# A recurrence with a gated feed-forward layer: another table for the order of its parts

## The chip, the cores and the metric

The kernel runs on one core of a Trainium2 chip. Its metric is the device time in microseconds (us) of one execution, taken as the median of several. Five engines work side by side, each through its own list of instructions, strictly in order: TensorE (PE, with PEld for the loading of its stationary operand), VectorE (DVE), ScalarE (ACT), GpSimd (POOL) and SyncE (SP), which issues every transfer of this kernel. An instruction whose input isn't there stops everything that stands behind it in the same list.

## What is computed

The first half is a linear-attention recurrence over 768 steps, for 4 batches of 8 heads with a head dimension of 40:

```python
for t in range(S):
    y[:, :, t] = einsum('bhd,bhde->bhe', r[t], state)
    Sa = einsum('bhde,bhe->bhd', state, a[t])
    state = state * w[t] - outer(Sa, b[t]) + outer(v[t], k[t])
```

The second half takes the result as rows of 320 values, x of shape (4, 768, 320):

```python
h = maximum(x @ w_in, 0)                 # 320 -> 1024
conv = a three-tap convolution of h along the sequence, per channel
out = (h * sigmoid(conv)) @ w_out        # 1024 -> 320
```

All of it is float32; inputs that arrive as 64-bit floats (the three weights) are turned into pairs of a high and a low part on the chip.

## The kernel before

The sequence is cut into 24 steps of 32 positions. Two steps make a pair (12 pairs, `pd`), for which the inputs w, a, k and b are loaded together, and two steps make a window of 64 positions (12 windows, `wd`) for the feed-forward layer. Within a step the recurrence is solved in closed form. The kinds of parts, each a Python generator whose `yield`s cut it into pieces, are:

- `weights` (token we, 23 parts, lines 208 to 320): loads a block of a weight matrix, turns it from 64-bit floats into a high and a low part with eight VectorE instructions (L217 to L235 on tiles such as `wo2q`), one ScalarE copy (L253) and one GpSimd subtraction (L255).
- `wakb`, `v`, `r` (ld, lv, lr): loads on the SP queue.
- `decays` and `decayed` (de, dd, one for each half of a pair): TensorE transposes w, a, k and b (L349), ScalarE shifts w into `wx` (L365, L366), VectorE scans it into running products `suf` and `pre` (L369, L376) and multiplies the transposed tiles into `ah`, `kt` and `bt` (L391, L399).
- `scores` and `hats` (sc, ha): TensorE products of the decayed tiles (L411), masked by VectorE into `at` (L437), and transposes back (L450).
- `solve_in` and `solve` (si, so, one for each pair): a triangular system of 32 unknowns is taken through DRAM into `bb` and solved by 31 pairs of instructions (L480 multiplies into `st`, L486 adds into `xx`). Pairs 0, 2, 4, 6, 8 and 10 are solved on VectorE, the odd ones on GpSimd. The result goes through DRAM into `tt` (L491, L496).
- `chain` (ch): the part that carries the state from step to step. TensorE multiplies the old state and v into `pp` (L514, L522), ScalarE copies it to `psb` (L527), TensorE applies the solution, `pu` (L533), ScalarE copies `u` (L538), TensorE builds the new state in `pn` (L549), VectorE adds the old one in four instructions (`s`, L562), and GpSimd scales it by the decay (L568).
- `rturn`, `vturn`, `uturn`, `sturn`, `pairs`, `outputs` and `finish` (rt, vt, ut, st, pa, ou, fi): the step's output. `pm` (L411) is masked by VectorE into `ms` (L614), `py` (L629, L638) is copied to `ysb` (L644), transposed to `pq` (L655) and multiplied by VectorE into `xf` (L657), which ScalarE and GpSimd split (L665, L667).
- `pack`, `moe_in` and `moe_out` (pk, mi, mo): the feed-forward layer. For each window there are four tiles `ph` of two blocks of 128 channels (16 matmuls, L700). ScalarE applies the maximum into `hb` (L714); VectorE copies the two columns at the border in from `hend` and out to it (L712, L716); ScalarE and VectorE do the three taps in `cc` (L721, L729), ScalarE the sigmoid (L734), VectorE the product (L736), ScalarE and GpSimd the split (L740, L743). Two tiles `po` of 24 matmuls (L754) follow for each window. `end` (en) does the last position.

The order of all this isn't left to a scheduler. The string `ORDER` at the top of the file is a list of tokens; `emit_all` reads it from left to right, and each token advances one part by one piece (`ch2` advances the chain of step 2 by one piece, `we13*2` weight block 13 by two). So a token's place fixes where its instructions stand in the list of every engine that it uses. `put` holds for each part what must have been issued before each of its pieces, and `advance` issues whatever is missing first; the semaphores that make the data safe come from the framework. There are 8 accumulator banks in TensorE's memory, six for the recurrence and two for the feed-forward layer.

```python
for token in ORDER.split():
    name, _, times = token.partition("*")
    numbers = [int(x) for x in name[2:].split(".") if x]
    for _ in range(int(times or 1)):
        advance((KINDS[name[:2]], *numbers))
```

Of the kernel before, what the change touches and what calls it, by code (L numbers as in the profile page):

```python
# [31 lines left out]
)  # L32

ORDER = """
    ld0 de0.0*2 ld0*2 de0.1 ld0 ld1 de0.1 we0 dd0.0*3 dd0.1*2 sc0 dd0.1 we0 ld1*2 lr0 sc0 sc1 lr1
    de1.0 sc1 ha0 de1.0 dd1.0 de1.1*2 we1*4 si0 ha0 ha1 dd1.0 we0*2 rt0 ld1 so0 ha1 dd1.0 so0 dd1.1
    ld2 so0*2 ld2 dd1.1 ld2 so0 dd1.1 ha2*2 sc2 ld2 lv0 lv1 vt0 ha3*2 so0*3 sc2 sc3 we2*2 sc3 we3
    we2*2 we3 we4 so0 we3*2 we5 we4 we5 si1 de2.0*2 ch0*4 we4*2 we6 lv2 de2.1*2 so1*2 ld3 ut0 pa0
    vt1 dd2.0*2 de3.0 we5 so1 we5 we7 ou0 we6 fi0 so1 dd2.0 ch1 we6 dd2.1 we7*2 ch1 we7 dd2.1*2 ld3
    st1*2 sc4 we6 so1 we8*4 we9 we10 ch1 lv3 rt1 we9 st1*2 ut1 pa1 lr2 ou1 ha4 ld3*2 we10 so1*3 fi0  # L40
    vt2 we10 fi0 fi1 de3.0 sc4 sc5 we9 we10 sc5 ch1 de3.1 we9 de3.1 ha4 we11 we12 lr3 rt2 fi1 st2*2
    fi1 we11 we12 we11*2 ro0 we13 we12*2 ha5 st2 we13 we14 ha5 ld4 so1 we13 dd3.0*3 dd3.1*3 we14*2
    ch2 si2 so2 ch2 pk0 ut2 so2*2 pa2 vt3 sc6 so2*2 st2 ou2 ch2 ro0 rt3 mi0.0*3 so2*2 mi0.0*2 ch2
    st3*2 we13 mi0.1*2 st3 ld4 so2 ld4 we14 lv4 we15 we16 ch3*2 sc6 sc7 ut3 we15 st3 we15 sc7 fi2*3
    lr4 mi0.0 pa3 mi0.0 ch3 we15 ch3 we16 mi0.0 we17 mi0.1 mi0.2 we17*2 mi0.2 so2 ch4 si3 we16 so3
    ou3 ha6 we16 we18 de4.0 we18 ha6 ha7 st4 fi3*2 we17 we19 de4.0 we18 mi0.1 we19 vt4 st4*3 lv5
    de4.1 ch4 ut4 so3 ch4 dd4.0 rt4 we18 we20 de4.1 we20 mi0.2 so3 we20 pa4 vt5 ch4 ch5 so3 mi0.2
    ch5 fi3 ha7 we19*2 we21*2 ut5 we20 we22*2 ou4 st5*2 mi0.1 st5 lr5 rt5 so3 we22 ld4 ld5 de5.0
    mi0.1 we21 ch5 we22 mi0.3 we21 mi0.0*2 so3 mi0.1*2 mi0.3 pa5 mi0.3 pk1 dd4.0*2 dd4.1 mi0.1*2
    dd4.1 st5 mi0.2 sc8 fi4*2 ld5 dd4.1 ou5 mi0.2 lv6 mi0.3 so3*2 sc8 mi0.2 sc9 mi0.2*2 ha8*2 ha9  # L50
    fi4 fi5 ld5 de5.0 de5.1 ha9 sc9 mi0.2 dd5.0 mi0.3 dd5.0 de5.1 lv7 mi1.0*3 mi1.1 ld5 dd5.0 dd5.1
    sc10 so3 si4 mi0.3 lr6 dd5.1*2 ch5 mi0.3 lr7 mi0.3 mi1.1*2 mi1.0*3 mi1.1 mi1.2 vt6 sc10 mi0.3
    mo0.0 sc11 mi0.3 mi1.1 mi1.0*2 mi1.1 ch6 st6 mi1.2 ch6*2 sc11 mi1.1*2 mo0.0*2 ch6 mo0.0 mo0.1*5
    ld6 ut6 rt6 ch7 mi1.1 so4 ld6 so4*2 pa6 vt7 st6 fi5*2 st6 so4*2 mi1.0 so4 mi1.2 st6 mi1.3 so4
    mi1.2 so4 lv8 ou6 mi1.0 mo1.0 mi1.2 mi1.3*2 st7*2 ch7 ut7 mi1.1 st7*2 rt7 ch7*2 mo1.0 pa7
    mi1.3*2 fi6*2 pk2 lr8 mi1.2*2 ou7 mi1.2 rt8 so4 si5 ch8 st8*2 mi1.2 mi1.3 mi1.2 mi1.3 ch8*2 lv9
    fi6 mi2.0*2 lr9 ld6 ch8 ha10*2 fi7 mi1.3*2 ha11 ld6 de6.0 vt8 lv10 de6.0 dd6.0 fi7 mi2.0 mi1.3
    mi2.1 ch9 mo1.0 mi2.0*2 de6.1 ch9 de6.1 so5*2 mi2.1 so5 mi2.0 ut8 mi2.1*4 mi2.0 mo0.0 mo1.0*2
    mo1.1 ha11 mi2.0 mi2.1 mo1.1 dd6.0 mo1.1 dd6.0 pa8 vt9 mo1.1 mi2.0*2 dd6.1 so5 fi7 st8*2 mi2.1*2
    dd6.1 so5 ou8 rt9 mi2.2 sc12 mi2.2*2 mi2.3*3 ut9 dd6.1 st9 mi2.1 mi2.2 ch9 mi2.2 mi2.3*2 mi2.2*2  # L60
    ld7 de7.0 lr10 ld7*2 so5*3 pa9 ch9 lr11 st9*3 pk3 ld7 mi2.3 mi2.2 mi3.0*2 mi2.3 mi3.0 mi2.3 fi8
    so5 fi8 mi2.2*2 mi2.3 mi3.0 ou9 mi3.1 fi8 sc12 fi9 de7.0 dd7.0 sc13 mo2.0*2 sc13 de7.1*2 mi3.1*2
    rt10 ha12*2 ha13 dd7.0 ha13 dd7.0 mi2.3 mi3.0 dd7.1*3 ch10 mi3.1*2 mi3.0 mi3.1 st10 fi9 mo2.0*2
    mo2.1 ch10*3 mo2.1 mi3.0 st10 mi3.1 st10*2 mi3.0 mi3.1 ut10 si6 so6 mi3.2*2 so6 lv11 vt10 mi3.2
    pa10 vt11 so6 mo1.1 so6 mi3.3 mo2.1 mi3.3 ch11 mo2.0 mo2.1 ld8 mi3.0 lr12 so6 ch11 so6 ou10 rt11
    mi3.3 mi3.1 ut11 pa11 st11*3 ld8 lv12 so6 mi3.2 mi3.3 st11 so6 sc14 ch11 vt12 mi3.1 lr13 sc14
    mi3.0 mo3.0 mi3.2 sc15 mi3.2 ch11 mi3.2 fi9 fi10 mi3.3 fi10*2 ou11 st12 ha14 sc15 mi3.2*2 mi3.3
    pk4 so6 ch12 mi3.2 de8.0 mi4.0*2 mi3.3 fi11*2 mi3.3 ch12*2 mo3.0 mi3.3*2 ch12 mi4.0*2 ut12 si7
    so7*2 mi4.1*2 fi11 mi4.1*2 lv13 mi4.0 ha14 st12 ha15 st12*2 mi4.0 mo3.0*2 mo3.1 mi4.1 rt12
    mi4.1*2 mi4.2 mo3.1 pa12 mo2.1 mo3.1*2 de8.0 so7 ld8 ch13 mi4.0*2 vt13 mi4.0*2 de8.1 dd8.0 mi4.2  # L70
    ou12 rt13 so7*2 mi4.2*2 mo3.0 so7*3 ch13 mi4.3 ld8 mi4.1*3 mi4.3 ld9 ch13 ha15 ut13 lv14 mi4.3
    pk5 mo3.1 fi12 de8.1 lr14 fi12 dd8.0*2 de9.0 dd8.1 ld9 dd8.1*2 sc16 mi4.2 st13*4 ld9*2 pa13
    mi5.0 mi4.2*3 mi5.0*2 mi4.2 mi5.0 mi4.2 ch13 mi4.3 ou13 ha16*2 sc16 sc17 fi12 fi13 ha17*2 de9.0
# [929 lines left out]
```

## Time and profile before

| | before |
|---|---|
| median of 3 executions | 708.97 us (708.5 to 709.71) |
| the profiled execution | 708.08 us |
| its span, from the first to the last instruction | 706.4 us |
| granted TensorE clock, mean | 0.906 |

The profile page and the answers of the trace come from that one execution. A row of the timeline gives the start in us from the span's start, how long it took, the engine, the line, the operation and its tiles without their numbers; in brackets behind it stands how long the engine sat idle just before, and who ended that wait. A row of the stretches gives, for a window of time, the busy time of each engine and the number of its instructions.

### The profile page before, as it was taken

Reading aid. Unit: us, or ns where it says so; the run is one execution under the profiler, and the core shown is the slowest. Engines: PE = TensorE matmul, PEld = TensorE weight load, DVE = VectorE, ACT = ScalarE, POOL = GpSimd, SP = SyncE. Lnnn points to the kernel's source line nnn. Section 1 sums busy time; section 2 is a strip of 40 time slices with the busy share of each in tenths; the row PEclk is TensorE's granted clock in tenths of the full one; section 3 lists DMA queues with packets and bytes.
Section 4 is the critical chain, followed back from the end, with each engine's and each line's share of the span. In section 5 each row is a group of like instructions: output and inputs, shape, how many; then the busy total and the mean of one; then the engine's idle time right before and its main releaser. Section 6 shows DMA issues by size and latency. Waiting matters only on the chain. (4 is left out here: it accounts for less than half of the span.)

```text
span 706.4 us, 29930 instructions
## 1 busy us (share of the span) xinstructions
PE 560.7 (79%) x13021; PEld 497.9 (70%) x13021; DVE 538.4 (76%) x1261; ACT 350.7 (50%) x792; POOL 353.2 (50%) x582
## 2 busy tenths in 40 slices
PE   4444764677687898988977996899998977899886
PEld 3334654566576787977866885789887876788775
DVE  6689889998999896657795578987979894456571
ACT  2322244254375455664454664466565546455651
POOL 2001884037786235783234884236985028863321
PEclk9766777997799998989999998999998999999998
DMA  8765456437125344544404446524435025121000
GB/s 139 120 117 108 103 112 102 95 94 144 22 41 107 56 72 79 94 81 82 82 20 89 86 86 106 81 60 69 89 62 91 6 54 94 29 51 32 21 30 19
DMA packets 242402, 53.40 MB, mean 76 GB/s; under 512 B 229000, under 2 KB 238112, under 8 KB 242272
## 3 DMA queue, kind: packets, MB, share of 16 engines
q1 hardware_dynamic: 242272, 51.50, 39.9%
q8 instruction: 102, 1.67, 1.0%
q14 instruction: 28, 0.23, 0.1%
HBM read 38.63 MB, written 10.22 MB: 69 GB/s over the span
## 5 line engine op out<-in xcount | busy, mean ns | idle before, releaser
L729 DVE SCALAR_TENSOR_TENSOR cc<-hb,cw,cc 128x256 f32<-128x256 f32 x192 | 106.3, 575 | 13.7 <-ACT cc L721 10.2
L568 POOL TENSOR_TENSOR s<-s,wc 120x360 f32<-120x360 f32 x88 | 75.8, 891 | 69.4 <-DVE s L562 69.4
L486 POOL TENSOR_TENSOR xx<-xx,st 128x126 f32<-128x126 f32 (+22 forms) x186 | 83.1, 447 | 14.6
L480 POOL TENSOR_TENSOR st<-xx,bb 128x126 f32<-128x126 f32 (+22 forms) x186 | 79.4, 427 | 21.1 <-DMA bb<-bd 8.4
L700 PE MATMUL ph<-xh,wih 120*128 120x256 f32 x288 | 56.6, 306 | 11.3 <-ACT hb L714 11.3
L486 DVE TENSOR_TENSOR xx<-xx,st 128x126 f32<-128x126 f32 (+22 forms) x186 | 54.2, 291 | 6.4
L480 DVE TENSOR_TENSOR st<-xx,bb 128x126 f32<-128x126 f32 (+22 forms) x186 | 53.6, 288 | 7.2 <-DMA bb<-bd 1.7
L736 DVE TENSOR_TENSOR cc<-cc,hb 128x512 f32<-128x512 f32 x48 | 40.8, 857 | 21.7 <-ACT cc L734 21.5
L562 DVE TENSOR_TENSOR s<-pn,s 120x360 f32<-120x360 f32 x88 | 40.6, 522 | 20.6 <-PE pn L549 20.6
L700 PEld LDWEIGHTS ph<-xh,wih 120*128 120x128 f32 x288 | 41.8, 194 | 15.0 <-ACT hb L714 13.1
L734 ACT ACTIVATE cc<-cc 128x512 f32<-128x512 f32 x48 | 30.4, 636 | 43.6 <-DVE cc L729 43.5
L667 POOL TENSOR_TENSOR xl<-xf,xh 120x384 fp32r<-120x384 f32 x24 | 26.8, 1117 | 45.2 <-ACT xh L665 41.5
L721 ACT ACTIVATE cc<-hb,cw 128x256 f32<-128x256 f32 x96 | 43.5, 506 | 8.7 <-DVE hb L712 2.9
L602 PE MATMUL pt<-ident,s 120*120 120x120 f32 x276 | 40.6, 279 | 6.4 <-DVE s L562 3.2
L427 ACT ACTIVATE ap<-ah,hmask 120x384 f32<-120x384 f32 (+1 forms) x72 | 36.6, 576 | 17.4 <-DVE ah L391 10.1
L604 ACT COPY sn<-pt 120x360 f32<-120x360 f32 x92 | 38.9, 471 | 12.2 <-PE pt L602 11.8
L714 ACT ACTIVATE hb<-ph 128x512 f32<-128x512 f32 x48 | 28.8, 600 | 27.2 <-PE ph L700 23.4
L579 ACT ACTIVATE rp<-pr,hmask 120x384 f32<-120x384 f32 x72 | 36.7, 586 | 6.9 <-PE pr L576 6.5
L700 PE MATMUL ph<-xl,wih 120*128 120x256 f32 x192 | 39.3, 287 | 0.0
L533 PE MATMUL pu<-psb,tt 32*32 32x40 f32 x1536 | 22.5, 209 | 19.6 <-ACT psb L527 16.1
L602 PEld LDWEIGHTS pt<-ident,s 120*120 120x120 f32 x276 | 31.2, 143 | 9.0 <-DVE s L562 3.5
L533 PEld LDWEIGHTS pu<-psb,tt 32*32 32x32 f32 x1536 | 18.7, 114 | 24.5 <-ACT psb L527 17.7
(867 smaller groups left out, 1665.9 us busy)
## 6 DMA issues: line engine op xcount, KB each, us to landing
bb<-bd SPq DMA_DIRECT2D x24, 256.0 KB
w<-in_w_dram SPq DMA_DIRECT2D x24, 160.0 KB
a<-in_a_dram SPq DMA_DIRECT2D x24, 160.0 KB
k<-in_k_dram SPq DMA_DIRECT2D x24, 160.0 KB
b<-in_b_dram SPq DMA_DIRECT2D x24, 160.0 KB
r<-in_r_dram SPq DMA_DIRECT2D x96, 40.0 KB
v<-in_v_dram SPq DMA_DIRECT2D x96, 40.0 KB
out_dram<-ob SPq DMA_DIRECT2D x22, 160.0 KB
```

The source lines that it names most:

```text
L480: eng.tensor_tensor(t3, xx[:, 0:nj, i : i + 1].to_broadcast([128, nj, nt]), bb[:, i : i + 1, i + 1 :].to_broadcast([128, nj, nt]), ALU.mult,)
L486: eng.tensor_tensor(xx[:, 0:nj, i + 1 :], xx[:, 0:nj, i + 1 :], t3, ALU.add)
L533: nc.tensor.matmul(pu[quad(bi), hc], tt[quad(bi), c, h, :], psb[quad(bi), hc], start=(h == 0), stop=True, skip_group_check=True,)
L562: nc.vector.tensor_tensor(new, pn[bi][:GR], old[bi], ALU.add)
L568: nc.gpsimd.tensor_tensor(n4, n4, w4, ALU.mult)
L579: nc.scalar.activation(out=rp[:, :, h, :], in_=pr[:GR], func=AF.Copy, scale=hmask[:, h : h + 1])
L602: nc.tensor.transpose(pt[:GR, g, :], old[bi][:, g, :], ident[:GR, :GR])
L604: nc.scalar.copy(sn, pt[:GR])
L700: nc.tensor.matmul(ph[:, j], l[:, fs], x, start=(j == 0 and i == 0), stop=(i == len(passes) - 1), skip_group_check=True,)
L721: nc.scalar.activation(out=cc[:, j], in_=hb[:, j, :, 1 : W + 1], func=AF.Copy, scale=cw[:, 1, f : f + 1],)
L729: nc.vector.scalar_tensor_tensor(out=cc[:, j], in0=hb[:, j, :, x : W + x], scalar=cw[:, x, f : f + 1], in1=cc[:, j], op0=ALU.mult, op1=ALU ...
L736: nc.vector.tensor_tensor(cc, cc, hb[:, :, :, 1 : W + 1], ALU.mult)
```

## The change

Only the string `ORDER` differs. Both strings hold the same tokens with the same counts, in another order, and the new one is two lines longer, so that every line number below it is two higher (L486 is L488 afterwards). No instruction, size, buffer count or other number differs; each engine has as many instructions as before. The whole table is rearranged, of which the first two lines show the manner:

```diff
-    ld0 de0.0*2 ld0*2 de0.1 ld0 ld1 de0.1 we0 dd0.0*3 dd0.1*2 sc0 dd0.1 we0 ld1*2 lr0 sc0 sc1 lr1
-    de1.0 sc1 ha0 de1.0 dd1.0 de1.1*2 we1*4 si0 ha0 ha1 dd1.0 we0*2 rt0 ld1 so0 ha1 dd1.0 so0 dd1.1
...
+    ld0 de0.0 ld0 de0.0 de0.1*2 ld0 dd0.0*2 ld0 dd0.0 dd0.1 sc0 dd0.1*2 we0*2 ld1 de1.0 sc0 sc1 ha0
+    sc1 lv0 we1 lv1 de1.0 de1.1*2 we1 ld1*3 dd1.0 ha0 ha1*2 si0 dd1.0 so0 dd1.0 so0 dd1.1 lr0 rt0
```

The tokens tell a reader little; the lists of the engines tell more. In the names below the first number is that of the step, pair or window, and what stands behind the underscore only tells buffers apart.

The first place is VectorE's list behind the last instruction of pair 2's solve (`xx2`, `st2_30`), about 149 us into the trace. Before, the list goes on with masks and a weight block:

```order
L486 TENSOR_TENSOR xx2_1736<-xx2_1736,st2_30_2105 128x16
L437 TENSOR_TENSOR at6_2207<-ps6_2208,trin_95 128x512
L217 TENSOR_SCALAR wo2q_2118<-wo2r_2117 128x256
L221 TENSOR_SCALAR wo2q_2118<-wo2r_2117 128x256
L225 SCALAR_TENSOR_TENSOR wo2q_2118<-wo2r_2117,wo2q_2118 128x256
L228 TENSOR_SCALAR wo2s_2119<-wo2r_2117 128x256
L230 SCALAR_TENSOR_TENSOR wo2q_2118<-wo2q_2118 128x256
```

Now the new state of step 3 (`s30` to `s33`) stands in its place:

```order
L488 TENSOR_TENSOR xx2_1919<-xx2_1919,st2_30_2267 128x16
L718 COPY hend_116<-hb00_2282 128x16
L439 TENSOR_TENSOR at6_2303<-ps6_2304,trin_95 128x512
L439 TENSOR_TENSOR at6_2303<-ps7_2334,trin_95 128x512
L564 TENSOR_TENSOR s30_2388<-pn30_2360,s20_1767 120x360
L564 TENSOR_TENSOR s31_2390<-pn31_2361,s21_1769 120x360
L564 TENSOR_TENSOR s32_2392<-pn32_2362,s22_1771 120x360
L564 TENSOR_TENSOR s33_2394<-pn33_2363,s23_1773 120x360
```

The same list reaches the state of step 4, the first that needs pair 2's solution, behind two weight blocks (wo1 and wo2), one `xf` and one `hend` after these; before, it stood behind five weight blocks, the tap products of a tile, a scan and more. The rows in front of step 4's state now are these:

```order
L219 TENSOR_SCALAR wo2q_2466<-wo2r_2465 128x256
L223 TENSOR_SCALAR wo2q_2466<-wo2r_2465 128x256
L227 SCALAR_TENSOR_TENSOR wo2q_2466<-wo2r_2465,wo2q_2466 128x256
L230 TENSOR_SCALAR wo2s_2467<-wo2r_2465 128x256
L232 SCALAR_TENSOR_TENSOR wo2q_2466<-wo2q_2466 128x256
L233 TENSOR_SCALAR wo2q_2466<-wo2q_2466 128x256
L234 SCALAR_TENSOR_TENSOR wo2q_2466<-wo2s_2467,wo2q_2466 128x256
L237 TENSOR_TENSOR wo2q_2466<-wo2q_2466 128x256
L564 TENSOR_TENSOR s40_2612<-pn40_2584,s30_2388 120x360
```

So the states of the steps have moved forward against the weight blocks.

The second place is VectorE's list around the last decayed tile of pair 6 (`bt6` from the transposed `pb61`), about 300 us into the trace. Before:

```order
L399 TENSOR_TENSOR kt6_5023<-pk61_5119,suf61_4917 120x6x2x32
L712 COPY hb22_5238<-hend_116 128x8x2
L712 COPY hb23_5258<-hend_116 128x8x2
L399 TENSOR_TENSOR bt6_5035<-pb61_5275,suf61_4917 120x6x2x32
L716 COPY hend_116<-hb22_5238 128x16
```

And now:

```order
L718 COPY hend_116<-hb22_4850 128x16
L401 TENSOR_TENSOR kt6_5137<-pk61_5165,suf61_4834 120x6x2x32
L731 SCALAR_TENSOR_TENSOR cc22_5172<-hb22_4850,cw_115,cc22_5172 128x256 x4
L738 TENSOR_TENSOR cc21_5090<-cc21_5090,hb21_4780 128x512
L714 COPY hb23_5307<-hend_116 128x8x2
L401 TENSOR_TENSOR bt6_5143<-pb61_5322,suf61_4834 120x6x2x32
```

Four tap products and a product of a tile have moved in between `kt6` and `bt6`.

TensorE's list in front of the transposition `pb61` at the same place, before:

```order
L700 MATMUL ph23_5249<-xl4_3292,wih_111 128x256 x2
L700 MATMUL ph23_5249<-xp2_4449,wil_112 128x256
L700 MATMUL ph23_5249<-xl4_3292,wil_112 128x256
L591 MATMUL put9_5269<-ident_80,u9_4915 120x128 x3
L349 MATMUL pb61_5275<-ident_80,b6_4763 120x128 x3
```

And now:

```order
L702 MATMUL ph23_5297<-xl4_3226,wih_111 128x256 x2
L702 MATMUL ph23_5297<-xp2_4315,wil_112 128x256
L702 MATMUL ph23_5297<-xl4_3226,wil_112 128x256
L351 MATMUL pb61_5322<-ident_80,b6_4742 120x128 x3
L413 MATMUL ps12_5328<-ap12_5259,kt6_5137 32x96 x8
```

Before, the tiles `ph22` and `ph23` of window 2, 32 matmuls, and the transposition `put9` stand right in front of `pb61`; now `ph22` has moved further ahead and `put9` behind.

More of the change, by code (lines that the diff above doesn't have):

```diff
@@ L40 @@
[L40 to L61, printed above, removed]
@@ new lines @@
+    mi1.1 mi1.2 lv8 ha9 mi1.0 dd5.0 so4 mi1.3*2 mi1.0 dd5.1 ld6*2 lv9 pk2 mi1.3 pa7 st7 so4*2
+    dd5.1*2 mi1.2 sc10 ch8 mi1.2 fi6 ou7 ha10*2 mi1.1 mi1.3 mi1.2 sc10 sc11 de6.0 mi2.0 mi1.3 sc11
+    mi1.2 mi2.0 fi6*2 mi1.3 mi2.0 fi7 mi1.2*2 ch8 mi1.3 ch8 mi1.3*2 mi2.0 si5 fi7 mi2.0 ch8 ld6*2
+    lr9 st8 mi2.1 mi2.0 vt8 lv10 mi2.1*3 mi2.0*2 fi7 so5 de6.0 de6.1 so5 de6.1 mi2.2*3 so5 ch9
+    mo1.0*4 mo1.1 mo1.0 rt8 mo1.1*2 mo0.1 dd6.0 ch9 mo1.1 mi2.0 st8*3 ch9 ut8 mi2.1 mo1.1 pa8 vt9
+    ha11*2 dd6.0*2 ld7 mi2.1 dd6.1 ld7 mi2.2 dd6.1 mi2.0 mi2.2 ou8 mi2.2 mi2.1 sc12 so5 rt9 so5
@@ L106 @@
+    mo11.1 mo11.0 mo11.1*2 en0 mo11.1*2 ch23 en0
 """
```

111 lines of the change are left out of this document (64 added, 47 removed).

## The prediction

> **What bounds the kernel now.** I read the stretches first, since shares over the whole span mix stages with different limits. The page's head gives VectorE 76% and TensorE 79%, so neither carries the kernel alone.
>
> ```profile
> PE 560.7 (79%) x13021; PEld 497.9 (70%) x13021; DVE 538.4 (76%) x1261; ACT 350.7 (50%) x792; POOL 353.2 (50%) x582
> ```
>
> Cut by stage, with the granted clock behind the five engines:
>
> ```profile
> 0.00:120.00 120.00, 60.85 (x1206) 51.27 (x1207) 99.29 (x257) 39.17 (x91) 47.43 (x99) 0.76 0.61 113
> 120.00:262.00 142.00, 113.44 (x2946) 99.66 (x2948) 127.95 (x316) 68.32 (x158) 66.24 (x107) 0.89 0.43 81
> 262.00:430.00 168.00, 145.31 (x3482) 129.57 (x3483) 118.33 (x258) 91.12 (x207) 103.18 (x174) 0.94 0.43 78
> 430.00:585.00 155.00, 138.84 (x3394) 124.95 (x3393) 134.10 (x311) 88.22 (x199) 76.54 (x109) 0.96 0.40 70
> 585.00:640.00 55.00, 47.91 (x1139) 43.17 (x1139) 23.22 (x49) 31.38 (x71) 42.27 (x80) 0.97 0.28 53
> 640.00:707.00 67.00, 54.33 (x865) 49.30 (x863) 35.51 (x74) 32.52 (x70) 17.56 (x16) 0.95 0.09 24
> ```
>
> Up to 262 us VectorE is the bound: from 120 to 262 us it is busy for 127.95 of 142 us. From 262 to 430 us nobody is full: VectorE is idle for 49.7 us (168 less 118.33), TensorE for 22.7 (168 less 145.31). Here order alone can cost time. From 430 to 585 us both are near 90%, and from 585 us on TensorE carries it.
>
> Next I took VectorE's timeline from 262 to 430 us, for the waits in brackets. These nine are its long ones:
>
> ```profile
> 261.19 0.18 DVE L486 TENSOR_TENSOR xx<-xx,st 128x16 f32<-128x16 f32 x1
> ...
> 273.26 1.85 DVE L562 TENSOR_TENSOR s<-pn,s 120x360 f32<-120x360 f32 x4 [3.29 <-PE pn L549]
> ...
> 278.11 1.43 DVE L369 TENSOR_TENSOR_SCAN suf<-wx,dsuf 120x384 f32<-120x384 f32 x1 [1.38 <-ACT wx L365]
> ...
> 285.84 0.96 DVE L369 TENSOR_TENSOR_SCAN suf<-wx,dsuf 120x384 f32<-120x384 f32 x1 [3.86 <-ACT wx L365]
> ```
>
> ```profile
> 303.27 0.56 DVE L399 TENSOR_TENSOR bt<-pb,suf 120x384 f32<-120x384 f32 x1 [5.05 <-PE pb L349]
> ...
> 307.28 2.33 DVE L729 SCALAR_TENSOR_TENSOR cc<-hb,cw,cc 128x256 f32<-128x256 f32 x4
> ...
> 312.12 0.85 DVE L736 TENSOR_TENSOR cc<-cc,hb 128x512 f32<-128x512 f32 x1
> ...
> 320.71 0.69 DVE L437 TENSOR_TENSOR at<-ps,trin 128x512 f32<-128x512 f32 x1 [5.43 <-PE ps L411]
> ```
>
> ```profile
> 340.10 1.85 DVE L562 TENSOR_TENSOR s<-pn,s 120x360 f32<-120x360 f32 x4 [2.54 <-PE pn L549]
> ```
>
> ```profile
> 382.59 1.85 DVE L562 TENSOR_TENSOR s<-pn,s 120x360 f32<-120x360 f32 x4 [4.59 <-PE pn L549]
> ...
> 388.24 0.17 DVE L716 COPY hend<-hb 128x16 f32<-128x16 f32 x1 [2.55 <-ACT hb L714]
> ...
> 406.01 0.39 DVE L716 COPY hend<-hb 128x16 f32<-128x16 f32 x1 [5.26 <-ACT hb L714]
> ```
>
> They add up to 3.29 + 1.38 + 3.86 + 5.05 + 5.43 + 2.54 + 4.59 + 2.55 + 5.26 = 33.95 us of the 49.7. In each, VectorE's list reached an instruction before TensorE's list had reached its producer.
>
> **The change, part by part.** No instruction is added or removed, so each stage moves only by waits and by work shifted across its border.
>
> *Up to 262 us.* The stage ends with the last instruction of pair 4's solve (261.19 us). In VectorE's list 569 instructions stand before it, and 572 in the new one. Seven have moved in (state 7's four, one `ms`, two border copies) and four out (two `at`, a `kt` and a `bt`): at their times in the trace 3.5 us against 2.5, so 1.0 us more. By the same count pair 6's solve has 1.0 us less before it than now, so that border cancels: zero. What may be lost here is a new wait. The new list pulls the states forward: between the end of pair 2's solve and state 4, which needs its solution, stand one `hend`, two `at`, state 3, two weight blocks, one `xf` and one `hend`. From start to start, these rows give their lengths:
>
> ```profile
> 148.01 0.17 DVE L716 COPY hend<-hb 128x16 f32<-128x16 f32 x1
> 148.13 0.21 DVE L480 TENSOR_TENSOR st<-xx,bb 128x45 f32<-128x45 f32 x1
> ...
> 149.37 0.68 DVE L437 TENSOR_TENSOR at<-ps,trin 128x512 f32<-128x512 f32 x1
> 149.97 0.28 DVE L217 TENSOR_SCALAR wo2q<-wo2r 128x256 int32<-128x256 int32 x1
> ...
> 152.62 0.68 DVE L437 TENSOR_TENSOR at<-ps,trin 128x512 f32<-128x512 f32 x1
> 153.22 0.55 DVE L657 TENSOR_TENSOR xf<-pq,pre 120x384 f32<-120x384 f32 x1
> 153.69 3.03 DVE L729 SCALAR_TENSOR_TENSOR cc<-hb,cw,cc 128x256 f32<-128x256 f32 x4
> ...
> 157.24 1.83 DVE L562 TENSOR_TENSOR s<-pn,s 120x360 f32<-120x360 f32 x4
> 159.00 0.53 DVE L217 TENSOR_SCALAR wo3q<-wo3r 128x256 int32<-128x256 int32 x1
> ```
>
> So 0.13 + 2 x 0.60 + 1.76 + 2 x 2.65 + 0.47 + 0.13 = 9.0 us. How long a state takes behind its solve is seen twice where VectorE waited for it: pair 4's solve ended at 261.37 us and state 8 began at 273.26, 11.9 us; pair 6's ended at 365.85 us and state 12 began at 382.59, 16.7 us.
>
> ```profile
> 365.66 0.19 DVE L486 TENSOR_TENSOR xx<-xx,st 128x16 f32<-128x16 f32 x1
> ```
>
> A wait of 2.9 to 7.7 us follows, where before state 4 came at 179.47 us, some 30 us behind the solve, and waited for nothing:
>
> ```profile
> 179.47 1.85 DVE L562 TENSOR_TENSOR s<-pn,s 120x360 f32<-120x360 f32 x4
> ```
>
> Behind it the weight blocks and decays queue on the engine that bounds the stage. I take +2.9 us, since the 16.7 us hold a slower load of the solution than pair 4's; the low end is 0, if the transfers go as fast as they can, the high end +7.7.
>
> *From 262 to 430 us.* For each of the nine waits I counted in both tables how much VectorE work stands ahead of the waiting instruction, and how much TensorE work ahead of its producer (VectorE's at its times in the trace, TensorE's at the usual distance of two starts, 0.12 us in these rows).
>
> ```profile
> 300.73 0.28 PE L700 MATMUL ph<-xh,wih 120*128 120x256 f32 x1
> 300.85 0.28 PE L700 MATMUL ph<-xh,wil 120*128 120x256 f32 x1
> ```
>
> If VectorE's side has grown by more than TensorE's, the wait is shorter by the difference, at most by all of itself. Take `bt6`, which waited 5.05 us at 303.27. Ahead of it, VectorE now has 4.8 us more (278.9 against 274.1), four tap products (2.33 us) and a product (0.85) among it; TensorE has 1.9 us more ahead of `pb61` (164.1 against 162.2). So 2.9 us of the wait are covered. In their order the nine give 1.4, 1.4, 3.9, 2.9, 2.2, 2.5, 0, 2.0 and 5.3: 21.6 us. That isn't what the end gains. A wait saved lets VectorE arrive earlier at its next wait, which grows by as much unless TensorE is earlier too; and TensorE waits for VectorE in between. The new table has its own tight places: `kt6`, `bt6`'s first half and step 9's `ms` now stand within a microsecond of where state 9 was tight before, and the tightest place of the stretch has eased by 1.0 us only, that around 406 us by 2. So the gain lies between 3 us (those two) and 21.6. I choose 7, a third of the whole, because the nine lie in two strings with less than 20 us between neighbours (six from 273 to 340 us, three from 382 to 406), and a string of waits pays little more than once. It is a choice, and the largest in this sum.
>
> *From 430 us on.* The places that were tight before are eased or tightened by 1 to 5 us, as many one way as the other; I take zero, with 5 us to either side. The last 296 instructions of TensorE's list are the same ones in the same order, from 661.10 us to the end, so the last 45 us keep their length:
>
> ```profile
> 661.10 0.65 PE L411 MATMUL pm<-rp,vt 120*32 120x96 f32 x24
> ```
>
> The sum against the profiled execution, 708.08 us (span 706.4, and 1.7 around it): +2.9 - 7 + 0 = -4.1, so 704.0 us. The median of the runs lies 0.9 us above that execution, so I forecast 704.9.
>
> By the Trainium skill's page "TensorE: Matmul & The Clock Gate" (What's actually happening), TensorE falls to half its clock after an idle window of some 3.4 us and regains it after a busy one. Fewer idle gaps from 262 to 430 us would by that rule also raise the 0.94 granted there; at the 0.97 of the stretch from 585 us, 145.31 us of work would take about 4.5 us less, an estimate which would put the time near 700.
>
> **The rivals.**
>
> *Slower: the recurrence pulled too far forward.* State 4 takes the 16.7 us of state 12, VectorE stands for 7.7 us in the stretch that it bounds, and the nine waits pay only 3: 708.08 + 7.7 - 3 + 0.9 = 713.7. It decides as soon as the latency behind a solve passes 9.0 us by more than what the later stretch gives. For it: before 262 us TensorE's granted clock is lowest (0.76 and 0.89) and the transfers' share is high (0.61 and 0.43). Against it: two solves' latencies are all I have, and the shorter was measured nearer.
>
> *Slower: VectorE and GpSimd in each other's way.* The product L736 shows it, one shape with these times (minimum, median, maximum in ns):
>
> ```profile
> L736 DVE TENSOR_TENSOR cc<-cc,hb x48: 678/692/1655, 163.0 to 689.7; 128x512 f32<-128x512 f32 x48
> ```
>
> The 40.8 us of its 48 calls are 8.3 more than 48 x 0.678. If the new neighbours double that on the path, -4.1 + 8.3 = +4.2, and 708.08 + 4.2 + 0.9 = 713.2.
>
> ```profile
> L736 DVE TENSOR_TENSOR cc<-cc,hb 128x512 f32<-128x512 f32 x48 | 40.8, 857 | 21.7 <-ACT cc L734 21.5
> ```
>
> The Trainium skill's page "SBUF — State Buffer" (Who interferes with whom) says that a VectorE instruction with two inputs in SBUF and a GpSimd one take a shared port pair in turn, whole instructions at a time. The spread of L736, which has two such inputs, agrees with it.
>
> *No change.* The waits move on: +2.9 - 3 = -0.1, and 708.9. For it: work per engine is the same, and TensorE from 430 us on is at 90%.
>
> *Much faster.* All nine covers pay: +2.9 - 21.6 = -18.7, and 690.3. TensorE's idle 22.7 us there would have to vanish nearly whole, so I allow little.
>
> That the change doesn't do what it says is excluded by the lists: each engine has the same instructions.
>
> **How the numbers follow.** I call a difference under 0.2% (1.4 us) none, about what a measurement of this kernel can tell. Forecast: 0.45, with a range of its own from 697 to 707.4 (the nine waits paying 14 down to 5). Much faster, 690 to 697: 0.12. No change: 0.16. Recurrence too far forward: 0.20. Ports: 0.07. So faster is 0.45 + 0.12 = 0.57, same 0.16, slower 0.20 + 0.07 = 0.27. The range from 692 to 715 holds both slower cases at their worked values with a little above, and leaves out the lower part of the much faster one, some 0.07, and as much at the top.
>
> **What would show it.** If right, the nine waits from 262 to 430 us sum to some 15 to 27 us, state 4 waits about 3 us for `pn`, pair 4's solve ends at about 264 us, the tail from step 23's `pm` takes 45 us again. State 4 waiting over 6 us shows the first rival; a sum of VectorE over 545 us busy, with L736 well over 45, the second. I'm wrong altogether if the difference arises behind 430 us, or before 120.

## The result: 3.5% slower

| | before | after |
|---|---|---|
| median (4 runs each) | 709.34 us (708.5 to 710.17) | 734.75 us (731.4 to 736.97) |
| the profiled execution | 708.08 us | 731.4 us |
| its span | 706.4 us | 729.7 us |
| granted TensorE clock, mean | 0.906 | 0.899 |

The ratio is 1.0354, with a 95% interval from 1.0312 to 1.0397. I had forecast 704.9 us, with a range up to 715. Sign and size are wrong. All medians and ratios below are of fast executions; five slow ones (one of `e3`, one of `e10`, two of `e11`, one of before) are left out.

The first part of the page of after (busy time, share of the span and count of each engine) says that the work is the same: TensorE is busy for 564.6 us (560.7 before), VectorE for 539.8 (538.4).

```profile
PE 564.6 (77%) x13021; PEld 498.6 (68%) x13021; DVE 539.8 (74%) x1261; ACT 351.9 (48%) x792; POOL 354.0 (49%) x582
```

So nearly all of the 23.3 us of span are idle time. The stretches of after, in the same columns as those of before:

```profile
0.00:120.00 120.00, 62.22 (x1315) 50.12 (x1319) 97.62 (x252) 38.93 (x91) 45.18 (x97) 0.75 0.66 115
120.00:262.00 142.00, 109.26 (x2660) 95.45 (x2652) 123.39 (x300) 62.55 (x141) 69.47 (x110) 0.84 0.39 75
262.00:430.00 168.00, 144.95 (x3584) 128.50 (x3582) 120.51 (x272) 95.58 (x217) 98.49 (x168) 0.97 0.45 79
430.00:585.00 155.00, 132.86 (x3206) 119.98 (x3206) 127.19 (x293) 84.76 (x191) 78.36 (x110) 0.98 0.39 69
585.00:640.00 55.00, 42.38 (x911) 38.68 (x910) 23.78 (x56) 24.96 (x56) 33.48 (x66) 0.91 0.21 41
```

Three stretches got through less than before: VectorE does 300 instructions from 120 to 262 us (316 before), TensorE 3206 from 430 to 585 (3394) and 911 from 585 to 640 (1139), there at a clock of 0.91 (0.97). From 262 to 430 us, where I expected the gain, VectorE does 272 (258 before) and TensorE 3584 (3482) at 0.97 (0.94).

The waits that I counted in that stretch did go. This is VectorE's timeline of after, its waits there and pair 4's last instruction:

```profile
270.00 0.18 DVE L488 TENSOR_TENSOR xx<-xx,st 128x16 f32<-128x16 f32 x1
...
282.67 1.85 DVE L564 TENSOR_TENSOR s<-pn,s 120x360 f32<-120x360 f32 x4 [3.01 <-PE pn L551]
...
305.47 1.85 DVE L564 TENSOR_TENSOR s<-pn,s 120x360 f32<-120x360 f32 x4 [7.74 <-PE pn L551]
...
317.50 0.56 DVE L401 TENSOR_TENSOR bt<-pb,suf 120x384 f32<-120x384 f32 x1 [0.63 <-PE pb L351]
...
318.82 0.69 DVE L439 TENSOR_TENSOR at<-ps,trin 128x512 f32<-128x512 f32 x1 [0.76 <-PE ps L413]
...
398.21 0.39 DVE L718 COPY hend<-hb 128x16 f32<-128x16 f32 x2 [2.67 <-ACT hb L716]
...
407.16 0.56 DVE L393 TENSOR_TENSOR ah<-pa,pre 120x384 f32<-120x384 f32 x1 [3.68 <-PE pa L351]
...
420.55 1.85 DVE L564 TENSOR_TENSOR s<-pn,s 120x360 f32<-120x360 f32 x4 [3.72 <-PE pn L551]
```

Of the nine, state 8 still waits 3.01 us, `bt6` 0.63, `at12` 0.76, tile 1 of window 4 2.67, and the rest nothing: 7.1 us instead of 33.95. New ones stand beside them: state 9 (7.74 us, 0.94 before), an `ah` (3.68) and state 13 (3.72).

Ahead of that, state 4, at which I expected a wait of 2.9 us, began at 167.51 us without one, 13.9 us behind the end of pair 2's solve at 153.62. VectorE waited earlier, at step 3's mask and at state 3, and behind, for a sigmoid at 262.52 us; pair 4's solve ended at 270.18 us, not at 264:

```profile
143.42 0.69 DVE L616 TENSOR_TENSOR ms<-pm,tri 128x512 f32<-128x512 f32 x1 [3.70 <-PE pm L413]
...
153.43 0.19 DVE L488 TENSOR_TENSOR xx<-xx,st 128x16 f32<-128x16 f32 x1
...
157.08 1.85 DVE L564 TENSOR_TENSOR s<-pn,s 120x360 f32<-120x360 f32 x4 [1.56 <-PE pn L551]
...
167.51 1.85 DVE L564 TENSOR_TENSOR s<-pn,s 120x360 f32<-120x360 f32 x4
...
262.52 0.69 DVE L738 TENSOR_TENSOR cc<-cc,hb 128x512 f32<-128x512 f32 x1 [3.66 <-ACT cc L736]
```

The largest loss lies behind 430 us, where I had put zero (the runs below show it). Two places there show a form that it takes. At the first, VectorE stands for 6.58 us until TensorE transposes k of pair 9 (`pk`):

```profile
446.06 0.56 DVE L401 TENSOR_TENSOR kt<-pk,suf 120x384 f32<-120x384 f32 x1 [6.58 <-PE pk L351]
```

TensorE's timeline shows why `pk` is late. Its list reached the next tile (`ph`), whose bank wasn't free, and stood for 6.38 us:

```profile
440.47 1.01 PE L702 MATMUL ph<-xh,wih 120*128 120x256 f32 x3 [6.38 <-ACT hb L716]
...
442.61 0.47 PE L756 MATMUL po<-woh,g41l 128*128 128x320 f32 x1
442.87 0.47 PE L756 MATMUL po<-wol,g41h 128*128 128x320 f32 x1
...
445.53 0.49 PE L351 MATMUL pk<-ident,k 128*120 128x128 f32 x3
```

And ScalarE's shows why the bank wasn't free. The copy `hb` that frees it took 0.59 us, but stood behind the split `g43h`, which waited 3.71 us for a VectorE product; and VectorE had two sets of scans to do ahead of that product:

```profile
439.30 0.62 ACT L742 CAST g43h<-cc 128x512 fp32r<-128x512 f32 x1 [3.71 <-DVE cc L738]
439.82 0.59 ACT L716 ACTIVATE hb<-ph 128x512 f32<-128x512 f32 x1
```

So VectorE works while TensorE stands, and then TensorE works while VectorE stands.

This place isn't wholly new. Before has one of the same form at the next tile: an `hb` copy stood behind a sigmoid that had waited 7.05 us for VectorE, and TensorE stood for 4.55 us, with a clock of 0.50 in the 5.11 us behind it. After has no gap at that tile.

```profile
436.15 0.63 ACT L734 ACTIVATE cc<-cc 128x512 f32<-128x512 f32 x1 [7.05 <-DVE cc L729]
...
437.74 0.60 ACT L714 ACTIVATE hb<-ph 128x512 f32<-128x512 f32 x1 [0.16 <-DVE cc L736]
```

```profile
438.39 1.01 PE L700 MATMUL ph<-xh,wih 120*128 120x256 f32 x3 [4.55 <-ACT hb L714]
```

Against before, TensorE's gap here has grown by 1.8 us only; what is new is that VectorE then stands for 6.58 us, where its longest wait from 430 to 448 us was 1.37.

The second place, at 591 us, has the same form, and before has no gap at its `po`. ScalarE's list has the sigmoid of window 8's tile 0, which waits for VectorE's taps, ahead of the copy `ob`; TensorE's next output tile `po` needs the bank that `ob` frees; VectorE's `xf` waits for TensorE:

```profile
589.75 0.63 ACT L736 ACTIVATE cc<-cc 128x512 f32<-128x512 f32 x1 [3.51 <-DVE cc L731]
...
591.09 0.40 ACT L773 COPY ob<-po 128x320 f32<-128x320 f32 x1
```

```profile
591.54 0.64 PE L756 MATMUL po<-woh,g70h 128*128 128x320 f32 x1 [5.78 <-ACT ob L773]
...
594.91 0.81 PE L657 MATMUL pq<-ident,ysb 128*120 128x128 f32 x3
```

In the list of waits, VectorE's total for `xf` rose from 10.9 to 33.3 us. The row of before, and that of after:

```profile
DVE xf L657 <- PE pq L655: 10.9, 9, 3.0
```

```profile
DVE xf L659 <- PE pq L657: 33.3, 11, 7.0
```

### The profile page after: what moved, and what is told of

It reads as the page before. It is cut to its first block, busy times and chain, and to the rows that moved or that the text cites. A ratio compares the mean times of both kernels' runs of the same rounds, so it can differ in the third digit from the quotient of the medians.

```text
span 729.7 us, 29918 instructions
## 1 busy us (share of the span) xinstructions
PE 564.6 (77%) x13021; PEld 498.6 (68%) x13021; DVE 539.8 (74%) x1261; ACT 351.9 (48%) x792; POOL 354.0 (49%) x582
## 5 line engine op out<-in xcount | busy, mean ns | idle before, releaser
L731 DVE SCALAR_TENSOR_TENSOR cc<-hb,cw,cc 128x256 f32<-128x256 f32 x192 | 112.3, 606 | 10.5 <-ACT cc L723 7.1
L570 POOL TENSOR_TENSOR s<-s,wc 120x360 f32<-120x360 f32 x88 | 79.4, 934 | 52.7 <-DVE s L564 52.7
L488 POOL TENSOR_TENSOR xx<-xx,st 128x126 f32<-128x126 f32 (+22 forms) x186 | 83.1, 447 | 14.6
L488 DVE TENSOR_TENSOR xx<-xx,st 128x126 f32<-128x126 f32 (+22 forms) x186 | 54.4, 293 | 6.4
L702 PEld LDWEIGHTS ph<-xh,wih 120*128 120x128 f32 x288 | 42.7, 198 | 19.4 <-ACT hb L716 16.9
L738 DVE TENSOR_TENSOR cc<-cc,hb 128x512 f32<-128x512 f32 x48 | 38.3, 798 | 20.0 <-ACT cc L736 19.9
L723 ACT ACTIVATE cc<-hb,cw 128x256 f32<-128x256 f32 x96 | 43.7, 509 | 13.2 <-DVE hb L714 4.1
L736 ACT ACTIVATE cc<-cc 128x512 f32<-128x512 f32 x48 | 30.3, 632 | 38.9 <-DVE cc L731 38.8
L659 DVE TENSOR_TENSOR xf<-pq,pre 120x384 f32<-120x384 f32 x24 | 13.2, 551 | 33.3 <-PE pq L657 33.3
L551 PE MATMUL pn<-v,khat 32*120 32x120 f32 x552 | 29.7, 319 | 8.6 <-DVE xf L659 3.7
```

The source lines that it names most:

```text
L488: eng.tensor_tensor(xx[:, 0:nj, i + 1 :], xx[:, 0:nj, i + 1 :], t3, ALU.add)
L570: nc.gpsimd.tensor_tensor(n4, n4, w4, ALU.mult)
L702: nc.tensor.matmul(ph[:, j], l[:, fs], x, start=(j == 0 and i == 0), stop=(i == len(passes) - 1), skip_group_check=True,)
L723: nc.scalar.activation(out=cc[:, j], in_=hb[:, j, :, 1 : W + 1], func=AF.Copy, scale=cw[:, 1, f : f + 1],)
L731: nc.vector.scalar_tensor_tensor(out=cc[:, j], in0=hb[:, j, :, x : W + x], scalar=cw[:, x, f : f + 1], in1=cc[:, j], op0=ALU.mult, op1=ALU ...
L738: nc.vector.tensor_tensor(cc, cc, hb[:, :, :, 1 : W + 1], ALU.mult)
```

## The experiments

My theory from here on, "local knots": the loss is a sum of separate places, at each of which an instruction of one engine that waits for a second one stands ahead of what a third one needs. Its first rival, "drift": the early part sets the recurrence back, and all later waits follow from that. Each kernel is a table of the same 1520 pieces. "Above before" is its median less that of before on the same chip; after itself is 25.4 us above. Line numbers in the rows differ by one or two from those of before. A mixed table takes the first pieces in one order and the rest in the other.

**Cut in parts.** First the table's head (525 pieces, up to pair 4's solve) put back, and the head alone:

```diff
# e1
-first 525 pieces: after
+first 525 pieces: before
 the rest: after
# e2
 first 525 pieces: after
-the rest: after
+the rest: before
```

> The first 525 of the 1520 pieces in the order of before, the rest in the order of after. Theory 'local knots' (the loss is the sum of separate places where the engines' lists lock into one another: about 6 to 8 us up to 262 us, 7 around 446, 11 between 590 and 640): only the first loss goes, 727 us (724 to 730). Rival 'drift' (the early part sets the recurrence back and the later waits only follow from that): nearly all goes, 709 to 714 us.

> The first 525 pieces in the order of after, the rest in the order of before. Local knots: only the early loss shows, 715 to 718 us. Drift: the later waits come as well, over 725 us. My prediction's own sum for this part (a wait of 2.9 us at state 4, nothing else): 712 us.

Measured: 725.38 us without the head (16.9 above before; ratio 1.0229, 1.0186 to 1.0271), 713.03 us with the head alone (4.5 above; 1.0075, 1.004 to 1.0109). Drift is out: with the old head, two thirds of the loss remain. Then the middle alone, pieces 526 to 843, from which my prediction took 7 us, and the tail alone:

```diff
# e8
 first 525 pieces: before
-pieces 526 to 843: before
+pieces 526 to 843: after
 the rest: before
# e11
 first 843 pieces: before
-the rest: before
+the rest: after
```

> Before, with the pieces 526 to 843 (about 262 to 427 us) in the order of after and everything else as before: the part from which my prediction took 7 us (range 3 to 21.6). Prediction: 701.5 us. By the comparison of the two traces, in which the nine waits of this stretch went but as many new ones came: 705 us, between 703 and 709. If the stretch lost time in truth: over 710.

> Before up to piece 843 (about 427 us), then the order of after. Local knots (the tail's loss doesn't depend on what stands before it): the 24 us that lie between 725.4 and 701.4, so 731 to 734 us. Rival 'the tail only loses because the middle gained' (state and loads come earlier and wait for others): under 725.

Measured: the middle 701.41 us (6.8 below before; 0.9909, 0.9873 to 0.9946), the tail 729.19 us (19.5 above; 1.0282, 1.0231 to 1.0334). The middle alone gives what I had taken from it, and is the fastest table of all. Its stretch shows in what form (before has 145.31 us of TensorE for 3482 matmuls at 0.94 there):

```profile
262.00:430.00 168.00, 144.67 (x3563) 129.39 (x3563) 121.90 (x267) 90.27 (x205) 103.99 (x173) 0.97 0.46 82
```

TensorE does 81 matmuls more in the same busy time, at 0.97, and VectorE nine instructions more; VectorE's idle time there fell only from 49.7 to 46.1 us. Head, middle and tail alone add up to 4.5 - 6.8 + 19.5 = 17.2 us, against 25.4 for the whole: 8 us more than the sum, and the head costs more on top of the other two (25.4 - 16.9 = 8.5) than by itself. What the parts do to each other is not settled.

**The two places of the tail.** One ScalarE instruction is moved in each; all other engines keep their lists.

```diff
# e3
-ld9 mi5.0 mi4.3*2 ld10 so7 mi5.0*2 mi5.1*2
+ld9 mi5.0 mi4.3 ld10 so7 mi5.0*2 mi4.3 mi5.1*2
# e4
-pa19 mi8.0*3 sc23 mi8.1 mo7.0 mo7.1*2
+pa19 mi8.0*2 sc23 mi8.1 mo7.0 mi8.0 mo7.1*2
```

> After, with one ScalarE instruction moved: the split of the gated tile 3 of window 4 (g43h, which waits for a VectorE product behind two scans) stands behind the copy hb50 that frees TensorE's accumulator bank, not ahead of it. Local knots: TensorE's 6.4 us gap at 440 us and VectorE's 6.6 us wait for pk90 at 446 us shrink by about 4.5 us each, 729 to 731 us. Rival 'recurrence order' (VectorE's place for kt9 is wrong, not ScalarE's for g43h): the wait stays within 2 us, 734 us.

> After, with one ScalarE instruction moved: the sigmoid of tile 0 of window 8 (which waits 3.5 us for VectorE's taps) stands behind the copy ob70 that frees TensorE's accumulator bank, not ahead of it. Local knots: TensorE's 5.8 us gap at 591.5 us shrinks to about 2, the xf waits of VectorE at 595.8 and 603 us shrink by 3 to 4, 730 to 732 us. Rival 'xf stands too early on VectorE': VectorE's waits keep their length and the time stays at 734 us.

Measured: 725.93 us (17.4 above before, 8.0 less than after; 1.0264, 1.0194 to 1.0334) and 728.63 us (20.1 above, 5.3 less; 1.0287, 1.0239 to 1.0335). The runs of the first spread widely, from 722.59 to 733.33 us, and each interval still overlaps that of after; the traces decide. TensorE's timeline with `g43h` moved:

```profile
433.55 0.62 PE L702 MATMUL ph<-xh,wih 120*128 120x256 f32 x3 [2.03 <-ACT hb L716]
...
434.75 0.31 PE L756 MATMUL po<-woh,g41l 128*128 128x320 f32 x1
434.90 0.31 PE L756 MATMUL po<-wol,g41h 128*128 128x320 f32 x1
...
436.44 0.49 PE L351 MATMUL pk<-ident,k 128*120 128x128 f32 x3
```

The gap is 2.03 us instead of 6.38, 4.35 less. And the same matmuls from `ph` to `pk` take 2.89 us (433.55 to 436.44), where behind the long gap they took 5.06 (440.47 to 445.53): two neighbours of `po` start 0.15 us apart here, 0.27 there. In after the place takes 4.35 + 2.17 = 6.5 us more than with `g43h` moved. VectorE's `kt` waits 0.48 us instead of 6.58:

```profile
436.97 0.56 DVE L401 TENSOR_TENSOR kt<-pk,suf 120x384 f32<-120x384 f32 x1 [0.48 <-PE pk L351]
```

With the sigmoid moved, TensorE's gap is 1.81 us instead of 5.78, and the twelve matmuls up to `pq` take 1.87 us (584.86 to 586.73) instead of 3.37 (591.54 to 594.91). But part of it is given back 20 us later, at a wait for a transfer that took 2.38 us in after:

```profile
584.86 0.41 PE L756 MATMUL po<-woh,g70h 128*128 128x320 f32 x1 [1.81 <-ACT ob L773]
...
586.73 0.49 PE L657 MATMUL pq<-ident,ysb 128*120 128x128 f32 x3
...
604.71 0.55 PE L702 MATMUL ph<-xp,wil 120*128 120x256 f32 x1 [4.00 <-DMA xp<-xh]
```

**A third place of the tail**, where TensorE's `py` waits 3.9 us at 648.5 us for VectorE's mask behind taps:

```diff
-lv22 mi9.1*2 st21 ch21 mi9.0 mi9.1*3 pa21 ou21 fi20
+lv22 mi9.1 st21 ch21 mi9.0 pa21 mi9.1 ou21 mi9.1*3 fi20
```

> After, with four pieces of window 9's tile 1 moved: its tap products stand behind the mask ms21 on VectorE, not ahead of it, and its sigmoid, product and split behind step 21's ysb. TensorE's gap of 3.9 us in front of py21 at 648.5 us should shrink to about 1, and its half-speed stretch behind it with it: local knots 730 to 732 us. Rival 'the tail's waits only move to xf21 or to state 21': 734 us.

Measured: 732.94 us (24.8 above before; 1.0351, 1.0307 to 1.0395). In the trace the wait went to 0.78 us, but the runs don't tell the time from that of after: too small to be shown.

**All three with the old head.**

```diff
 e1, with the moves of e3, e4 and e6
```

> The head in the order of before (first 525 pieces), the rest in the order of after with the moves of g43h, of sig80 and of window 9's tile 1 together. Local knots add up: 725.4 less 6.5, less 6, less 3, about 710 us (706 to 713). Rival 'untied knots overlap' (each move gives back part of another's gain): 716 to 720 us.

Measured: 709.77 us (1.6 above before; 1.0028, 0.9996 to 1.0059). Against the 16.9 us of the old head alone, six moved pieces gave back 15.3. The knots add up (alone, the moves gave 8.0, 5.3 and 0.6). But this says what undoing them is worth in the new order, and not that they are the whole of what it lost: the first place stands in before in its own form, with a gap of 4.55 us, and no run undoes it there. Against the middle alone, 1.6 + 6.8 = 8.4 us of the tail are left, without a named place that I could undo. I tried one: here TensorE stood for 5.3 us at 594 us for the transfer of `xp`.

```diff
-mi8.3*2 mi9.0*2 mi8.3 mi9.0 mi8.2*2 mi8.3 ut20
+mi8.3*3 mi8.2*2 mi8.3 ut20
 ...
-vt21 st20*3 ch21
+vt21 st20*3 mi9.0*3 ch21
```

> The kernel with the head of before and three places untied (709.8 us), with one more: the first matmuls of window 9 (ph90), which stood for 5.3 us at 594 us for the transfer of xp, go behind the products of step 20's output, which were ready. Local knots: the gap falls to about 2 and the time by 3.5 to 5, 705 to 706 us. Rival 'TensorE waits for step 20's chain anyway': 709 to 711.

Measured: 712.06 us (2.4 above before; 1.0036, 1.0002 to 1.0069): no gain. The matmuls that I put in front had a knot of their own. TensorE now waits for `vt`, and ScalarE's list has a sigmoid and a split for VectorE's taps ahead of that copy:

```profile
595.71 1.08 PE L412 MATMUL pm<-rp,vt 120*32 120x96 f32 x24 [7.89 <-ACT vt L594]
```

```profile
593.76 0.63 ACT L735 ACTIVATE cc<-cc 128x512 f32<-128x512 f32 x1 [1.67 <-DVE cc L730]
...
595.17 0.48 ACT L594 COPY vt<-pvt 120x384 f32<-120x384 f32 x1
```

**The head.** Up to the end of VectorE's 577th instruction, just behind pair 4's solve, VectorE is busy for 230.0 us in before and 230.5 in after, and idle for 34.8 and 41.9 (added up from its timeline). That instruction ends at 264.8 us, against 272.4 (262.8 to 264.4 and 270.6 to 272.5 in the other runs with the same head). First, two of its waits taken away by moving other parts of the recurrence:

```diff
-ut0 pa0 de2.0 ou0 de2.1 we5
+ut0 pa0 de2.0 de2.1 ou0 we5
 ...
-ut3 pa3 so2 st3 fi2 st3 ou3
+ut3 so2 st3 fi2 st3 pa3 ou3
```

> After, with two pieces of the early stretch moved: the transposition of w for the second half of pair 2 and its shift wx ahead of step 0's py and ysb (VectorE waited 3.7 us for that wx at 75.5 us), and step 3's mask ms3 behind eight solve instructions and one xf (VectorE waited 3.7 us for pm3 at 143.4 us). Local knots, with VectorE as the bound up to 262 us: both waits go nearly whole and the time falls by 4 to 6.5 us, 728 to 731. Rival 'slack later': the stretch gives it back in its next waits (the state of step 3, the product cc11 at 262.5), 733 to 735.

Measured: 734.98 us (26.8 above before; 1.0375, 1.0337 to 1.0412). Nothing gained, as the rival had it: the wait for `wx` went, but the next one (for a GpSimd subtraction) grew from 3.18 to 3.59 us, and the 3.70 us in front of `ms3` became 1.93 there and 2.02 at a mask behind it, and state 3 still began at 156.67 us:

```profile
102.57 0.80 DVE L230 TENSOR_SCALAR wi13s<-wi13r 120x256 int32<-120x256 int32 x1 [3.59 <-POOL wil L257]
...
144.40 0.69 DVE L616 TENSOR_TENSOR ms<-pm,tri 128x512 f32<-128x512 f32 x1 [1.93 <-PE pm L413]
154.34 0.69 DVE L439 TENSOR_TENSOR at<-ps,trin 128x512 f32<-128x512 f32 x1 [2.02 <-PE ps L413]
156.67 1.85 DVE L564 TENSOR_TENSOR s<-pn,s 120x360 f32<-120x360 f32 x4 [1.64 <-PE pn L551]
```

Then the waits filled with work that has to be done anyway, two weight blocks:

```diff
-ut3 pa3 so2 st3
+ut3 we14 pa3 so2 we15 st3
 ...
-sc7*2 ch3 we14 ha6
+sc7*2 we15 ch3 ha6
 ...
-rt4 we15*2 lv4
+rt4 lv4
```

> After, with VectorE's instructions of two weight blocks moved forward: wo1 (2.65 us) ahead of the mask ms3, where VectorE waited 3.7 us, and wo2 (2.65 us) ahead of state 3, where it waited 2.1 us in two waits; their loads go ahead with them. Theory 'recurrence too far forward at steps 2 and 3' (the list ahead of a state that is bound by its own chain is too short, and only other work put there fills the wait): about 4.5 us of the head's idle time go, 729 to 731. Rival 'the head's idle time is set elsewhere' (as when the two waits were taken away without other work and came back): 733 to 735.

Measured: 732.71 us (23.1 above before; 1.0338, 1.0294 to 1.0381), 2.3 less than after, within the uncertainty. The waits at `ms3` and state 3 went, and state 4 now has one of 6.25 us. Pair 2's solve ends at 151.88 us, so state 4 takes 13.2 us behind its solve, between the 11.9 and 16.7 that I had read for two later pairs:

```profile
151.69 0.19 DVE L488 TENSOR_TENSOR xx<-xx,st 128x16 f32<-128x16 f32 x1
...
165.11 1.85 DVE L564 TENSOR_TENSOR s<-pn,s 120x360 f32<-120x360 f32 x4 [6.25 <-PE pn L551]
```

Last the sigmoid for which VectorE waited 3.66 us at 262.5 us, moved ahead of two copies on ScalarE, on top of the blocks:

```diff
 with the blocks of e9
-mo0.1*3 mi1.2 mi1.3 st7 mi1.1 lr8 mi1.1
+mo0.1*3 mi1.1 mi1.2 mi1.3 st7 lr8 mi1.1
```

> After, with the two weight blocks forward as in the run with wo1 and wo2, and with one ScalarE instruction moved: the sigmoid of tile 1 of window 1, which was ready at 256.5 us but stood behind the copy hb12 and a copy sn that waited for TensorE until 261.5, goes ahead of both. VectorE waited 3.7 us for it at 262.5 us. Local knots: that wait goes, pair 4's solve ends 3 to 4 us earlier than with the blocks alone, and the head has lost almost nothing against before: 728 to 730 us. Rival 'the wait comes back at state 8, which is bound by the solve's way through memory': 732 to 733 with a longer wait there.

Measured: 732.28 us (22.1 above before; 1.0296, 1.0257 to 1.0334), 3.3 less than after with both moves. The wait went, and a `bt` waits in its place, at 261.75 us, 2.93 us for TensorE's `pb`.

To find where the head loses, I cut it in three, each third alone in before:

```diff
# e15
+pieces 1 to 179: after
# e16
+pieces 180 to 312: after
# e17
+pieces 313 to 525: after
```

> Before, with only the first 179 pieces (to about 122 us) in the order of after. The readout is the end of VectorE's 577th instruction, behind pair 4's solve: 264.8 us in before, 270.6 to 272.5 in six runs with the whole head of after. If the head's loss lay in its waits at 75 and 102 us, the end here is 270 or later; if those are given back (the two lists meet again at 118 us, 1.5 us apart), 265 to 267, and the time 708 to 711.

> Before, with the pieces 180 to 312 (about 122 to 200 us) in the order of after, where states 2 to 4 are pulled forward. If the loss is made here: the 577th instruction ends at 269 to 271, the time is 713 to 716. If it is made behind 200 us: 265 to 266.

> Before, with the pieces 313 to 525 (about 200 to 262 us) in the order of after. If the loss is made here: the 577th instruction ends at 269 to 271. If it is made by the states pulled forward before 200 us: 264 to 266, and the time 708 to 711.

Measured, with the end of the 577th instruction (264.8 us in before, 272.4 in after): 713.58 us (4.6 above before; 1.0048, 1.0017 to 1.0079) and 266.5; 713.44 us (4.5 above; 1.0054, 1.0022 to 1.0086) and 268.5; 716.75 us (7.8 above; 1.0117, 1.0028 to 1.0207) and 273.6. All three lose, the last most, and together 16.9 us, where the whole head alone costs 4.5. Each cut adds a border that neither table has, so these don't add up; the head's loss is spread, and which waits make it is not settled.

**All moves together, in after.**

```diff
 after, with the moves of e3, e4, e6, e9 and e12
```

> After with all of the moves together: wo1 and wo2 forward, the sigmoid 11 forward, g43h behind hb50, sig80 behind ob70, window 9's tile 1 behind ms21. If the loss is a sum of such places: 734 less 5 (head), less 6.5, less 6, less 1, about 715 us (711 to 719). Rival 'the places overlap, or the rest of the table loses by itself': over 721.

Measured: 719.33 us (9.2 above before; 1.0107, 1.0066 to 1.0148). Ten moved pieces of 1520 give back 16.2 of the 25.4 us, just short of what the local knots let expect.

**On top of the fastest table**, three ScalarE instructions moved behind those for which TensorE stood 3.2 us at 593.7 us:

```diff
 with the table of e8
-ch21 mi8.2*3 st20*2 mi8.3 so11 vt20 lv22 mi8.3 ut20 rt20 lr21 lr22 pa20
+ch21 mi8.2*3 mi8.3 so11 vt20 lv22 ut20 rt20 lr21 lr22 pa20 st20*2 mi8.3
```

> Before with the middle of after (701.4 us), and three ScalarE instructions (two copies sn of step 20 and the centre tap cc of tile 3 of window 8) moved behind vt, ut, rp and rt of step 20, in front of which TensorE stood for 3.2 us at 593.7 us. Local knots: the gap falls by about 1.7 us, and the time by 2 to 3, 699 us. Rival 'TensorE then waits for sn in py20': 701.

Measured: 705.1 us (5.1 below before; 0.992, 0.9886 to 0.9953). No gain over the 0.9909. The gap fell from 3.19 to 2.31 us, and TensorE then waits 0.86 us for `sn` in `py`, as the rival had it.

## Why the prediction was wrong

1. *From 430 us on: zero, with 5 us to either side.* This is the step that failed. The tail alone costs 19.5 us. I had said that the difference arising behind 430 us would show me wrong altogether, and it does. I weighed two lists at a time, VectorE's against TensorE's, and only at places that were tight in before. The waits that the runs undid go through a third list: a ScalarE copy that frees a bank, behind a ScalarE instruction that waits for VectorE. ScalarE is half idle on the page (48%), so I never laid its list beside the others. Moving one of its instructions at a time, without touching TensorE's or VectorE's order, gave back 8.0 and 5.3 us. Open stays how much of the first is loss against before, which has a gap of 4.55 us at the next tile, and what makes the 8.4 us that are left of the tail.
2. *Pair 4's solve: counts cancel, and a new wait of 2.9 us at state 4.* Right sign, wrong place, too small. The counts did cancel (230.0 against 230.5 us of VectorE work), but the head costs 4.5 us alone and 8.5 on top of the rest, in waits that don't stand at state 4. The 9.0 us of list that I put between pair 2's solve and state 4 took 13.9, of which 2.1 were the waits at a mask and at state 3, so the solution was there in time. Where work was put in front of step 3's mask and state 3, the wait came to state 4, at a latency of 13.2 us. Moves there gave back 3.3 us at most, which the intervals don't tell from nothing.
3. *From 262 to 430 us: -7.* Right: -6.8 by itself, with an interval of some 4 to 9 us. That it came so near is luck, since 7 was a choice between 3 and 21.6. Of the 21.6 us of covers, most were real (the nine waits sum to 7.1 us in after), and a third of them paid. That the rest moves on to other waits held too (state 9, 7.74 us). VectorE's idle time fell by 3.6 us only; on TensorE's side the granted clock rose from 0.94 to 0.97, the value that I had put beside the rule of the Trainium skill's page "TensorE: Matmul & The Clock Gate".
4. *The last 45 us keep their length.* They took 46.8 us, from `pm` of step 23 at 682.91 us to the end, 1.5 us more than before.
5. The rival *recurrence too far forward* had the head right in kind (states pulled forward wait for their chain) and named the smaller part of the loss. *Port sharing* is out as the cause: VectorE is busy for 539.8 us, not over 545, and the product L736 (L738 now) fell from 40.8 to 38.3 us. The taps (L729, L731 now) rose from 106.3 to 112.3 us, but VectorE's whole busy time rose by 1.4 us only.

## What to carry to other kernels

Where the order of several in-order lists changes, check every list that stands between two others, the half-idle one first: for each copy that frees a bank or a buffer, look at what stands ahead of it and on whom that waits. Places that have slack before are no evidence for after, since a new order makes new tight places; a forecast that goes by the old tight places doesn't see them. A place that a run undoes with profit may stand in the old kernel too, so look there before its worth is counted as loss. To locate a loss spread over a whole table, splice the two tables at points where they hold nearly the same pieces, and time each part alone.

## What the runs showed of the hardware

A gap of TensorE can cost more than its length. Behind gaps of 6.38 and 5.78 us matmuls of one shape started 0.27 us apart, behind gaps of 2.03 and 1.81 us 0.15 apart, in the same lists; that made 2.2 and 1.5 us on top of the gap, up to the next instruction that somebody waited for. The granted clock of these four stretches was 0.52 and 0.50 behind the long gaps, and 1.00 behind the short ones. The Trainium skill's page "TensorE: Matmul & The Clock Gate" (What's actually happening) gives half the clock behind an idle window of about 3.4 us, and says that this window runs free. These four gaps agree.

The length of the gap alone doesn't decide, though. In after's TensorE timeline a gap of 2.38 us, shorter than the page's window, with one of 0.42 right behind it, is followed by slow matmuls (0.42 us, where the same form takes 0.28 in the row ahead of the gap), at a clock of 0.50 from 612.60 to 616.00 us:

```profile
608.55 0.28 PE L702 MATMUL ph<-xh,wil 120*128 120x256 f32 x1
...
611.45 0.36 PE L702 MATMUL ph<-xp,wil 120*128 120x256 f32 x1 [2.38 <-DMA xp<-xh]
...
612.93 0.42 PE L702 MATMUL ph<-xh,wil 120*128 120x256 f32 x1
```

And one gap went both ways. In the table with the middle of after, TensorE stands for 3.19 us ahead of `pm`; the clock in the 3.33 us behind the gap was 1.00, and the second row of `pm` took 0.62 us:

```profile
593.67 0.65 PE L412 MATMUL pm<-rp,vt 120*32 120x96 f32 x24 [3.19 <-ACT rp L580]
```

In before, at the same place of the list, the gap is 3.18 us; the clock in the 4.03 us behind it was 0.58, and the second row took 0.91 us:

```profile
600.17 0.65 PE L411 MATMUL pm<-rp,vt 120*32 120x96 f32 x24 [3.18 <-ACT rp L579]
600.64 0.91 PE L411 MATMUL pm<-rp,ut 120*32 120x96 f32 x24
```

A window that runs free would do this; what share of a window has to be idle, these runs don't show.
